# Batch 0's k and v: 128 partitions, one queue, and a compact kv

## The chip, the cores and the metric

The kernel runs on one core of a Trainium2 chip. The metric is the time of one execution on the device in microseconds (us); lower is better. Three executions of the kernel before took 262.84, 264.09 and 265.5 us, so the median is 264.09 us.

The engines of the core are named as the profile names them: PE multiplies matrices (PEld is its weight load), DVE works on vectors, ACT applies functions elementwise, POOL is a general engine, SP only issues transfers. DMA moves data between the device memory and the on-chip memory. A DMA that SP or ACT issues goes to a hardware queue (q1 for SP in the profile), one that POOL issues goes to the software queue q0; a cast from float32 to bfloat16 on the way is done only in POOL's DMAs here.

## The reference

For each of 8 batches and 8 heads with 576 tokens and head size 64, a linear attention is computed, and its output of 512 columns goes through a normalised two-layer block:

```python
q_s = softmax(q, over the 64 columns of a token)
k_s = softmax(k, over the 576 tokens)
kv  = einsum('bhsd,bhse->bhde', k_s, v)        # 64 x 64 for each head
x   = einsum('bhsd,bhde->bhse', q_s, kv)       # heads side by side: 576 x 512
xn  = (x - mean) / sqrt(var + 1e-6) * g_ln
out = x + relu(xn @ w_ch1) @ w_ch2             # 512 -> 2048 -> 512
```

Inputs and output are float32. The kernel multiplies in bfloat16 and accumulates in float32.

## The kernel before

The tokens of a batch are cut into four tiles of 128 (t = 0 to 3) and a remainder of 64; the remainders of all eight batches form a ninth block. Batches 1 to 7 and that ninth block are pipelined: while PE runs the two layers of one batch, the other engines prepare the attention of the next. The order of the instructions on every engine is written out by hand: a list of main steps (`mlp_steps`) with weights, and side steps with a place among them (`run`). Each engine works its own list strictly in order.

Batch 0 has nothing to hide behind, so `first_batch` (L957) handles it by itself:

- SP issues q's tiles 0 and 1 (L978) and then k in four transfers of two heads (L980). k and v stand on P0 = 96 partitions, with T0 = 6 tokens on each.
- POOL waits in its list at `gate` (L1004) for q's first transfer. Then it issues v with a cast (three DMAs, L1006), q's tiles 2 and 3 (two DMAs, L970 through L1010), and then the weights: the first 512 columns of w_ch1 in two halves of its rows (L1013), the other three blocks of 512 columns (L99), w_ch2, and batch 1's inputs. All of these share the software queue.
- PE keeps itself busy with products of a tile of zeros (`warm`, L867: 34, later 11 more).
- q's tiles 0 and 1 are exponentiated (L220), normalised on DVE (L229, L274, L923) and transposed through PE (L928) into `eqT`.
- k is exponentiated on ACT for two heads at a time (L293). Products with a column of ones give the sums of k (`z0_mm`, L306); products with v for two heads at a time give a 128 x 128 block with two useful 64 x 64 blocks on its diagonal (`kv0_mm`, L321). DVE divides by the sums and masks with `diag` in one instruction, which also sums the rows (L322); `mbc` spreads the sum divided by -512 over 128 columns (L327, L331).
- `xT_mm` (L342) gives x for tiles 0 and 1 already transposed and with the mean taken off: a direct part (one product of 128 rows for each pair of heads j) and a mean part (products with `mbc`). `xT_out` (L351, L353) scales it by g and writes `xnT`, the input of the first layer.
- The first layer (`mm1_part`, L520) starts with 8 products of the upper rows of w_ch1 (ko 0, 1) and goes on with 8 of the lower rows (ko 2, 3), each set over m = 0 to 3 for tiles 0 and 1. Side steps stand between: at 2 and 4 `q0_rest` for tiles 2 and 3 (sums of q by PE, L940, then x through PE with all of kv of batch 0, L414), at 6 the transpose of tile 2's normalised x (`xn_pT`, L928 and L932).

What matters for the order is that ACT's list holds exp of q's tiles 2 and 3 (L1039, L1040), then the scalings of `xT_out` 2 and 3.

Of the kernel before, what the change touches and what calls it, by code (L numbers as in the profile page):

```python
# [15 lines left out]
ALU = mybir.AluOpType  # L16
# [4 lines left out]
def kernel(  # L21
# [49 lines left out]

    ident = const.tile([P, P], BF16)
    eps_ln = const.tile([P, 1], FP32)
    gate = const.tile([P, 4], FP32)
    ones = const.tile([P, 1], BF16)
    junk = const.tile([P, 256], BF16)
    scrap = const.tile([P, 512], BF16)
    bones = const.tile([P, 2], BF16)
    ones_w = const.tile([P, P], BF16)
    diag = const.tile([P, P], FP32)  # L80
    mbc = const.tile([P, NP, P], BF16)
# [9 lines left out]
    vr = const.tile([P, 2, H, VW], BF16)  # L91
    vm = const.tile([P, 2, T, H, VW], BF16)

    w1_src = moe_w_ch1.rearrange("(ko ki) n -> ki ko n", ki=P)
    w2_src = moe_w_ch2.rearrange("(ko ki) n -> ki ko n", ki=P)

# [190 lines left out]
    kvbox = {}  # L287

    def exp_k0(j):
        hs = slice(2 * j, 2 * j + 2)  # L290
        if j == 0:
            eks[0] = raw.tile([P, T0, H, D], BF16, tag="kt", name="ek0", bufs=1)
        nc.scalar.activation(  # L293
            eks[0][0:P0, :, hs, :].rearrange("p t h d -> p h t d"), raws[0][0][0:P0, hs], AF.Exp
        )

    def k0_mm(j, t):
        hs = slice(2 * j, 2 * j + 2)
        return eks[0][0:P0, t, hs, :], raws["v0"][0:P0, hs, t, :], P

    def z0_mm(j):

        if j == 0:
            kvbox["z0"] = mm_ps.tile([P, NP], FP32, tag="m", name="z0")
        for t in range(T0):
            nc.tensor.matmul(  # L306
                kvbox["z0"][:, j : j + 1], k0_mm(j, t)[0], ones[0:P0],
                start=(j == 0 and t == 0), stop=(t == T0 - 1), skip_group_check=True,
            )

    def recip_z():
        kvbox["rz"] = sml.tile([P, NP], FP32, tag="rzk", name="rzk")
        kvbox["sum"] = sml.tile([P, NP], FP32, tag="lnv", name="kvs")
        nc.vector.reciprocal(kvbox["rz"], kvbox["z0"])

    def kv0_mm(j):
        pool, tag = (att_ps, "a") if j < 2 else (mm_ps, "m")
        pkv = pool.tile([P, P], FP32, tag=tag, name="pkv")
        for t in range(T0):
            lhsT, rhs, w = k0_mm(j, t)  # L320
            nc.tensor.matmul(pkv[:, 0:w], lhsT, rhs, start=(t == 0), stop=(t == T0 - 1))  # L321
        nc.vector.scalar_tensor_tensor(  # L322
            kv_sb[:, 0, j, :], in0=pkv, scalar=kvbox["rz"][:, j : j + 1], in1=diag,
            op0=ALU.mult, op1=ALU.mult, accum_out=kvbox["sum"][:, j : j + 1],
        )
        if j < NP - 1:
            nc.scalar.activation(  # L327
                mbc[:, j], ones_w, AF.Copy, scale=kvbox["sum"][:, j : j + 1]
            )
        else:  # L330
            nc.vector.tensor_scalar_mul(  # L331
                out=mbc[:, j], in0=ones_w, scalar1=kvbox["sum"][:, j : j + 1]
            )

    def xT_mm(j, kh):

        if j == 0:
            pobox["T", kh] = mm_ps.tile([P, 2, 2, P], FP32, tag="m", name="pxT")
        ops = [(kv_sb[:, 0, j, :], j % 2)] if j // 2 == kh else []
        ops += [(mbc[:, j], i) for i in range(2)]  # L340
        for n, (lhsT, i) in enumerate(ops):
            nc.tensor.matmul(  # L342
                pobox["T", kh][:, i], lhsT, eqTs[0][:, 0:2, j, :],
                start=(j == 0 and n == 0), stop=(j == NP - 1 and n >= len(ops) - 2),
                skip_group_check=True,
            )
# [8 lines left out]
    halves = (slice(0, 64), slice(64, P))  # L355

    def kv_pairs(b, ts=range(T + 1)):

# [598 lines left out]
    def first_batch():  # L957

        nc.scalar.preload_act_table_set("natural_log_exp_and_others")
        raws[0] = (  # L960
            mlp.tile([P, H, T0, D], FP32, tag="hT", name="kt0", bufs=1), None,
            raw.tile([P, H, T, D], FP32, tag="qt", name="qt"),
        )
        k0, _, q0 = raws[0]
        v0 = mlp.tile([P, H, T0, D], BF16, tag="hs", name="v0", bufs=1)
        raws["v0"] = v0

        def load_q0(t, tn, eng):
            ts = slice(t, t + tn)
            eng.dma_start(  # L970
                q0[:, :, ts],
                q[0, :, 0:SM, :].rearrange("h (p t) d -> p h t d", t=T)[:, :, ts],
            )

        def src0(x, h0, hn):
            return x[0, h0 : h0 + hn].rearrange("h (p t) d -> p h (t d)", t=T0)

        load_q0(0, 2, nc.sync)  # L978
        for h0 in range(0, H, 2):
            nc.sync.dma_start(  # L980
                k0[0:P0, h0 : h0 + 2].rearrange("p h t d -> p h (t d)"), src0(k, h0, 2)
            )
# [6 lines left out]
        nc.vector.memset(ones, 1.0)  # L989
# [3 lines left out]
        nc.vector.memset(ones_w, -1.0 / DM)  # L993
        nc.vector.memset(diag, 0.0)
        for ps in halves:
            nc.vector.memset(diag[ps, ps], 1.0)
        nc.vector.memset(kv_sb[:, 1:B], 0.0)
# [4 lines left out]
        make_identity(nc, ident)  # L1002
        nc.gpsimd.tensor_copy(out=ident_f, in_=ident[0:KO1, 0:KO1])
        nc.gpsimd.tensor_copy(out=gate, in_=q0[:, 1, 0, 0:4])  # L1004
        for h0, hn in ((0, 4), (4, 2), (6, 2)):
            nc.gpsimd.dma_start(  # L1006
                v0[0:P0, h0 : h0 + hn].rearrange("p h t d -> p h (t d)"), src0(v, h0, hn)
            )
        for t in range(2, T):
            load_q0(t, 1, nc.gpsimd)  # L1010
        for kh in range(2):
            ks = slice(2 * kh, 2 * kh + 2)
            nc.gpsimd.dma_start(w1_sb[:, ks, 0:512], w1_src[:, ks, 0:512])  # L1013
# [12 lines left out]
        warm(11)  # L1026
        eq_pT(0, 1, nc.vector)
        for j in range(NP):
            exp_k0(j)
            z0_mm(j)  # L1030
            if j == NP - 2:
                g_columns()
        recip_z()
        kv0_mm(0)
        kv0_mm(1)
        kv0_mm(2)
        xT_mm(0, 0)
        kv0_mm(3)
        exp_qt(0, 2)  # L1039
        exp_qt(0, 3)  # L1040
        xT_mm(1, 0)
        xT_mm(2, 0)
        xT_mm(0, 1)
        xT_mm(3, 0)
        xT_out(0)
        xT_out(1)
        eq_pT(0, 2, nc.scalar)
        xT_mm(1, 1)
        xT_mm(2, 1)
        eq_pT(0, 3, nc.vector)  # L1050
        xT_mm(3, 1)
        xT_out(2)
        xT_out(3)

    def q0_rest(t):
        z_q(0, t)
# [20 lines left out]
    def load_batch(b, parts=(2, 0), after=None):  # L1077
# [14 lines left out]
    with tc.manual_schedule(  # L1092
# [11 lines left out]
        def po_x(c, t):  # L1104
            for i in range(NP):
# [85 lines left out]
```

## Time and profile before

| What | Value |
|---|---|
| Median of three executions | 264.09 us (262.84 to 265.5) |
| Profiled execution, its own time | 265.09 us |
| Its span, first to last instruction | 263.3 us |
| PE busy | 254.8 us (97%) |
| DVE, ACT, POOL busy | 223.6, 177.7, 101.3 us |
| TensorE clock granted from 4.8 us to 264.2 us | full speed |
| DMA | 45.04 MB, mean 171 GB/s |

The span is less than the execution's own time by 1.8 us, which lie around the instructions. Times in a view count from the start of the span. A view by line names the line of the kernel and the tile that is written and read; a number behind x is how many instructions were merged; square brackets give how long the engine was idle before and what ended the wait. Busy shares say little here, because the first 20 us have other limits than the rest. The profile counts a casting DMA by the bytes that it writes, half of what it reads.

### The profile page before, as it was taken

The page shows a single profiled execution, that of the slowest core. Times are in us where ns is not written, and L with a number is a line of the kernel's source. Part 1 is how long each engine was busy: PE and PEld are TensorE (multiplying, and loading weights), DVE is VectorE, ACT ScalarE, POOL GpSimd, SP SyncE. Part 2 cuts the span into 40 slices and gives each one's busy share as a digit, 9 for nine tenths or more (in the row PEclk, how much of TensorE's full clock was granted, in tenths as well). Part 3 has the DMA queues.
Part 4 walks back from the last instruction along what each step waited for, and adds up shares of the span by engine and source line. Part 5 has one row for each costly group of instructions (what it writes and reads, how often), then busy time and mean ns, then how long its engine had stood idle before and what let it go on. Part 6 is the DMA issues. An engine that isn't in the chain of part 4 may idle for free.

```text
span 263.3 us, 7326 instructions
## 1 busy us (share of the span) xinstructions
PE 254.8 (97%) x2904; PEld 218.2 (83%) x2907; DVE 223.6 (85%) x544; ACT 177.7 (67%) x348; POOL 101.3 (38%) x158
## 2 busy tenths in 40 slices
PE   8879999999999999999999999999999999999993
PEld 6669854788888788888888888888988888888883
DVE  6658996998998999799979997999799979967873
ACT  4646972797887677688768866886688386638500
POOL 3952238240099306920790089008200910090000
PEclk9999999999999999999999999999999999999999
DMA  6999999987699997699879968998902540323014
GB/s 201 249 201 208 353 218 242 267 235 243 146 131 192 332 162 142 194 309 118 136 207 305 115 125 254 268 113 147 289 9 42 122 159 4 60 64 120 2 40 120
DMA packets 82618, 45.04 MB, mean 171 GB/s; under 512 B 58196, under 2 KB 79192, under 8 KB 82584
## 3 DMA queue, kind: packets, MB, share of 16 engines
q0 software_dynamic: 32464, 21.76, 44.8%
q1 hardware_dynamic: 49488, 22.29, 37.3%
q10 hardware_dynamic: 632, 0.53, 0.7%
q8 instruction: 22, 0.36, 0.6%
q14 instruction: 12, 0.10, 0.1%
HBM read 36.70 MB, written 9.44 MB: 175 GB/s over the span
## 4 chain that ended last, share of the span: by engine, by line
PE 91%; DMA 5%; POOL 2%; DVE 0%; issue 0%; DVEq 0%
PE ba L604 21%; PE bx L762 20%; PE bb L762 10%; PE ph L520 8%; PE bb L604 6%; PE be L604 5%; PE bc L604 5%; PE pc L556 5%; PE bc L762 5%; DMA w_raw<-in_moe_w_ch_dram 3%; PE pkv L371 2%; DMA qt<-in_q_dram 2%; PE po L403 2%; PE ptr L928 1%; PE po L414 1%; POOL v L1006 1%
## 5 line engine op out<-in xcount | busy, mean ns | idle before, releaser
L604 PEld LDWEIGHTS <-hs 128*128 128x128 bf16 x512 | 49.6, 98 | 6.3 <-issue 0.3
L269 POOL TENSOR_TENSOR tq<-xnT 128x256 bf16<-128x256 bf16 x30 | 20.1, 671 | 83.4 <-DMA xnT<-xn 42.5
L762 PEld LDWEIGHTS <-w_raw 128*128 128x128 bf16 x480 | 46.5, 98 | 6.4 <-issue 0.8
L604 PEld LDWEIGHTS <-hT 128*128 128x128 bf16 x392 | 37.6, 98 | 4.2
L762 PEld LDWEIGHTS <-w1g 128*128 128x128 bf16 x360 | 34.8, 98 | 4.2
L762 PE MATMUL bx<-tq,w_raw 128*128 128x256 bf16 x240 | 31.6, 273 | 0.3 <-DVE bb L793 0.3
L604 PE MATMUL ba<-w_q,hs 128*128 128x256 bf16 x256 | 30.6, 273 | 0.0
L786 ACT COPY bc<-bx 128x512 f32<-128x512 f32 x30 | 16.7, 596 | 19.1 <-PE bx L762 19.1
L427 ACT ACTIVATE scrap<-x,mv 128x512 bf16<-128x512 bf16 x32 | 23.1, 723 | 4.7 <-DVE mv L457 4.5
L793 DVE TENSOR_TENSOR bb<-bx,s 128x512 f32<-128x512 f32 x30 | 19.4, 694 | 7.7 <-ACT s L790 5.1
L804 ACT ACTIVATE hT<-bb 128x512 bf16<-128x512 f32 x30 | 16.4, 595 | 10.8 <-PE bb L762 10.8
L587 DVE TENSOR_TENSOR hs<-hT 128x1024 bf16<-128x1024 bf16 x32 | 21.3, 672 | 0.5 <-ACT hT L804 0.5
L796 DVE TENSOR_TENSOR hT<-bx,s 128x512 bf16<-128x512 f32 x30 | 19.3, 684 | 2.9 <-PE bx L762 2.7
L804 ACT ACTIVATE hT<-bc 128x512 bf16<-128x512 f32 x30 | 16.3, 595 | 7.8 <-PE bc L762 7.8
L229 DVE TENSOR_REDUCE zq<-eq 128x16 f32<-128x1024 bf16 (+1 forms) x20 | 20.7, 1050 | 0.6 <-ACT eq L220 0.5
L269 POOL TENSOR_TENSOR tq<-xnT,tq 128x256 bf16<-128x256 bf16 x30 | 20.0, 668 | 1.1
L449 DVE SCALAR_TENSOR_TENSOR x<-po,rq 128x256 bf16<-128x256 f32 x48 | 17.5, 420 | 1.4 <-PE po L403 1.4
L790 ACT COPY s<-bb 128x512 f32<-128x512 f32 x30 | 16.6, 623 | 0.0
L520 PE MATMUL ph<-xnT,w_raw 128*128 128x256 bf16 (+1 forms) x144 | 15.0, 261 | 1.5 <-DMA w_raw<-in_moe_w_ch_dram 1.5
L804 ACT ACTIVATE hT<-bx 128x512 bf16<-128x512 f32 x30 | 16.4, 610 | 0.0
L762 PE MATMUL bx<-xnT,w1g 128*128 128x256 bf16 x120 | 16.2, 273 | 0.0
L762 PE MATMUL bb<-xnT,w_raw 128*128 128x256 bf16 x120 | 15.8, 273 | 0.0
(156 smaller groups left out, 537.0 us busy)
## 6 DMA issues: line engine op xcount, KB each, us to landing
out_dram<-ot POOLq DMA_DIRECT2D x30, 256.0 KB, 4.6
kt<-in_k_dram SPq DMA_DIRECT2D x5, 1024.0 KB, 12.5
qt<-in_q_dram SPq DMA_DIRECT2D x4, 1024.0 KB, 8.6
qt<-in_q_dram POOLq DMA_DIRECT2D x2, 1024.0 KB, 13.2
kt<-in_k_dram POOLq DMA_DIRECT2D x2, 1024.0 KB, 14.2
vm<-in_v_dram POOLq DMA_DIRECT2D x16, 128.0 KB, 13.1
qt<-in_q_dram SPq DMA_DIRECT2D x3, 512.0 KB, 5.9
w_raw<-in_moe_w_ch_dram POOLq DMA_DIRECT2D x3, 512.0 KB, 11.8
```

The costliest lines, as they stand in the source:

```text
L229: nc.vector.reduce_sum(eqs[c][1][:, ts], eqs[c][0][:, ts], axis=AX.X)
L269: nc.gpsimd.tensor_tensor(out=dst[:, t], in0=x[:, t], in1=y[:, t], op=ALU.subtract)
L427: nc.scalar.activation(scrap, x[:, t], AF.Square, bias=mv[:, t, 0:1], scale=-float(DM), accum_out=mv[:, t, 1:2],)
L449: nc.vector.scalar_tensor_tensor(x[:, t].rearrange("p (i two d) -> p i two d", two=2, d=D)[:, :, half], in0=pobox[c, t][half], scalar=1.0, ...
L520: nc.tensor.matmul(ph[:, m % 2, at : at + tn], (w1g if c else w1_sb)[:, ko, m * P : (m + 1) * P], xnTs[c][:, t0 : t0 + tn, ko, :], start=( ...
L587: nc.vector.tensor_tensor(out=dst, in0=x, in1=y, op=op)
L604: nc.tensor.matmul(hbox[bank][:, t, cs], lhsT, rhs[:, cs], start=first and (own or t == 0) and k == 0, stop=k == KH - 1, skip_group_check= ...
L762: nc.tensor.matmul(dst[:, q], lhsT, rhs, start=first and q == 0 and ko == 0, stop=ko == 1, skip_group_check=True)
L786: nc.scalar.copy(at[g, "c"], at[g, "x"])
L793: nc.vector.tensor_tensor(out=at[g, "b"], in0=at[g, "x"], in1=at[g, "s"], op=ALU.add)
L796: nc.vector.tensor_tensor(out=h_out(g, 1, 1), in0=at[g, "x"], in1=at[g, "s"], op=ALU.add)
L804: nc.scalar.activation(h_out(g, odd, half), at[g, name], AF.Relu)
```

## The change

- k and v of batch 0 are laid out as 2 heads x 64 partitions with T0 = 9 tokens each, so on all 128 partitions, one pair of heads in a transfer. v arrives as float32 (`v0f`) and is cast on the chip: three pairs on ACT, one on DVE (`cast_v0`).
- SP issues everything of batch 0 on its one queue: q's tiles 0 and 1, k (4), v (4), then q's tiles 2 and 3 together. POOL's `gate` now waits for the last transfer of k, and its next DMA is the first of the weights.
- v has a 65th column of ones, so the products give the sums of k as well; `z0_mm` is gone. A product now takes one head's 64 partitions and 64 columns: 72 instead of 24.
- The three pairs of the first group are evicted together, the fourth by itself (`kv0_out`), to a compact `kvc` and the scaled sums `kvm`. ACT copies `kvc` to the diagonal of `kv_sb` later (`kv0_copy`). `diag`, `ones_w` and `mbc` are gone.
- x's direct part is two products of 64 rows for each pair (`xT_kv`); the mean part reads one column of `kvm` 128 times (`xT_mean`).
- `g_columns` stands right behind the 34 warm products. The clearing of `kv_sb` for batches 1 to 7 goes from DVE to POOL. The transpose of q's tile 2 is evicted by DVE, and tile 3's transposes stand in the first layer at 1. ACT's list becomes: exp of q (2), exp of k (4), casts (3), first copy of kv, exp of q's tile 2, `xT_out` 1, exp of q's tile 3, `xT_out` 3, second copy of kv.
- For batches 6 and 7 q and k are loaded in two halves; before, this was so for batch 7's q alone.

```diff
-    T0 = 6
-    P0 = S // T0
+    T0 = 9
...
+    def cast_v0(j, eng):
+        dst, src = raws["v0"][:, j, :, 0:D], raws["v0f"][:, j]
...
+    groups = (slice(0, NP - 1), slice(NP - 1, NP))
+
+    def kv0_mm(j):
...
         for t in range(T0):
+            for ps in halves:
+                nc.tensor.matmul(
+                    kvbox[n][ps, j - js.start], eks[0][ps, j, t], raws["v0"][ps, j, t],
...
+    def kv0_out(n):
...
+        nc.vector.reciprocal(rz, pkv[:, :, D])
+        if num > 1:
+            nc.vector.tensor_mul(kvc[:, js], pkv[:, :, 0:D], rz.to_broadcast([P, num, D]))
+            nc.vector.reduce_sum(total, kvc[:, js], axis=AX.X)
+        else:
+            nc.vector.scalar_tensor_tensor(
+                kvc[:, js.start], in0=pkv[:, 0, 0:D], scalar=rz, in1=ones_f,
+                op0=ALU.mult, op1=ALU.mult, accum_out=total,
+            )
+        nc.vector.tensor_scalar_mul(out=kvm[:, js], in0=total, scalar1=-1.0 / DM)
+
+    def kv0_copy(n):
+        for ps in halves:
+            nc.scalar.copy(kv_sb[ps, 0, groups[n], ps], kvc[ps, groups[n]])
+
+    def xT_kv(j):
...
+        for ps in halves:
             nc.tensor.matmul(
+                pobox["T", kh][ps, i], kvc[ps, j], eqTs[0][ps, 0:2, j, :],
...
+    def xT_mean(j, kh):
+        for i in range(2):
             nc.tensor.matmul(
+                pobox["T", kh][:, i], kvm[:, j : j + 1].to_broadcast([P, P]),
+                eqTs[0][:, 0:2, j, :], start=False, stop=(j == NP - 1), skip_group_check=True,
             )
...
-        if i < 2:
+        if i % 2 == 0:
             nc.vector.tensor_scalar_mul(out=dst, in0=src, scalar1=g_one[:, i : i + 1])
...
         load_q0(0, 2, nc.sync)
+        for x, dst in ((k, k0), (v, v0f)):
+            for j in range(NP):
+                nc.sync.dma_start(
+                    dst[:, j : j + 1].rearrange("p j t d -> p j (t d)"), src0(x, j, 1)
+                )
+        load_q0(2, 2, nc.sync)
...
+        nc.gpsimd.memset(kv_sb[:, 1:B], 0.0)
+        nc.gpsimd.tensor_copy(out=gate, in_=k0[:, NP - 1, 0, 0:4])
...
-        nc.gpsimd.tensor_copy(out=gate, in_=q0[:, 1, 0, 0:4])
-        for h0, hn in ((0, 4), (4, 2), (6, 2)):
-            nc.gpsimd.dma_start(
-                v0[0:P0, h0 : h0 + hn].rearrange("p h t d -> p h (t d)"), src0(v, h0, hn)
-            )
-        for t in range(2, T):
-            load_q0(t, 1, nc.gpsimd)
...
         warm(34)
+        g_columns()
...
+        for j, eng in enumerate((nc.scalar, nc.scalar, nc.vector, nc.scalar)):
+            cast_v0(j, eng)
+        for j in range(NP):
+            kv0_mm(j)
+            if j < NP - 1:
+                warm(2)
             if j == NP - 2:
+                kv0_out(0)
+        kv0_out(1)
+        for j in range(NP - 1):
+            xT_kv(j)
+        for j in range(NP):
+            xT_mean(j, 0)
+        kv0_copy(0)
         exp_qt(0, 2)
         xT_out(0)
         xT_out(1)
+        xT_mean(0, 1)
+        xT_mean(1, 1)
+        xT_mean(2, 1)
+        xT_kv(3)
+        xT_mean(3, 1)
+        exp_qt(0, 3)
         xT_out(2)
         xT_out(3)
+        eq_pT(0, 2, nc.vector)
+        kv0_copy(1)
...
-            hn = H // 2 if (b, which) == (B - 1, 2) else H
+            hn = H // 2 if b >= B - 2 else H
...
+                (1, lambda: eq_pT(0, 3, nc.vector)),
                 (2, lambda: (q0_rest(2), x_fast(0, 2), x_normed(2))),
```

More of the change, by code (lines that the diff above doesn't have):

```diff
@@ L78 @@
     bones = const.tile([P, 2], BF16)
-    ones_w = const.tile([P, P], BF16)
-    diag = const.tile([P, P], FP32)
-    mbc = const.tile([P, NP, P], BF16)
+    ones_f = const.tile([P, D], FP32)
+    gate = const.tile([P, 4], FP32)
+    kvm = const.tile([P, NP], BF16)
+    kvc = const.tile([P, NP, D], BF16)
     g_one = const.tile([P, KO1], FP32)
@@ L92 @@
     vm = const.tile([P, 2, T, H, VW], BF16)
+    halves = (slice(0, 64), slice(64, P))
     w1_src = moe_w_ch1.rearrange("(ko ki) n -> ki ko n", ki=P)
@@ L289, in exp_k0 @@
     def exp_k0(j):
[L290 removed]
         if j == 0:
[L292 to L305 removed]
+            eks[0] = raw.tile([P, NP, T0, D], BF16, tag="kt", name="ek0", bufs=1)
@@ new lines, in exp_k0 @@
+        nc.scalar.activation(eks[0][:, j], raws[0][0][:, j], AF.Exp)
+    def cast_v0(j, eng):
+        dst, src = raws["v0"][:, j, :, 0:D], raws["v0f"][:, j]
+        if eng is nc.scalar:
+            nc.scalar.copy(dst, src)
+        else:
+            nc.vector.tensor_copy(out=dst, in_=src)
+    groups = (slice(0, NP - 1), slice(NP - 1, NP))
+    def kv0_mm(j):
+        n, js = next((n, js) for n, js in enumerate(groups) if js.start <= j < js.stop)
+        if j == js.start:
+            kvbox[n] = att_ps.tile([P, js.stop - js.start, VW], FP32, tag="a", name="pkv")
+        for t in range(T0):
+            for ps in halves:
+                nc.tensor.matmul(
+                    kvbox[n][ps, j - js.start], eks[0][ps, j, t], raws["v0"][ps, j, t],
+                    start=(t == 0 and j == js.start), stop=(t == T0 - 1), skip_group_check=True,
+                )
@@ L306, in z0_mm @@
+    def kv0_copy(n):
+        for ps in halves:
+            nc.scalar.copy(kv_sb[ps, 0, groups[n], ps], kvc[ps, groups[n]])
+    def xT_kv(j):
+        kh, i = divmod(j, 2)
+        if i == 0:
+            pobox["T", kh] = mm_ps.tile([P, 2, 2, P], FP32, tag="m", name="pxT")
+        for ps in halves:
             nc.tensor.matmul(
-                kvbox["z0"][:, j : j + 1], k0_mm(j, t)[0], ones[0:P0],
-                start=(j == 0 and t == 0), stop=(t == T0 - 1), skip_group_check=True,
-            )
@@ L311, in recip_z @@
[L311 to L341, printed above, removed]
+                pobox["T", kh][ps, i], kvc[ps, j], eqTs[0][ps, 0:2, j, :],
+                start=(i == 0), stop=False, skip_group_check=True,
+            )
+    def xT_mean(j, kh):
+        for i in range(2):
@@ L992, in first_batch @@
         nc.vector.memset(bones[64:P, 1:2], 1.0)
[L993 to L997, printed above, removed]
+        nc.vector.memset(ones_f, 1.0)
+        nc.vector.memset(v0[:, :, :, D:], 1.0)
+        nc.vector.memset(kv_sb[:, 0], 0.0)
+        make_identity(nc, ident)
+        nc.gpsimd.tensor_copy(out=ident_f, in_=ident[0:KO1, 0:KO1])
+        nc.gpsimd.memset(kv_sb[:, 1:B], 0.0)
+        nc.gpsimd.tensor_copy(out=gate, in_=k0[:, NP - 1, 0, 0:4])
         nc.vector.memset(vr, 0.0)
```

52 lines of the change are left out of this document (15 added, 37 removed).

## The prediction

> **What bounds the kernel now.** I first read the chain of work that ended last, in its first 36 us (start, us, what):
>
> ```profile
> 0.74 4.38 DMA qt<-in_q_dram
> ...
> 5.17 0.19 POOL gate L1004
> 5.36 2.07 POOL v L1006 x3
> 7.43 1.84 POOL qt L970 x2
> 9.27 0.64 POOL w_raw L1013
> 9.91 8.81 DMA w_raw<-in_moe_w_ch_dram
> 18.72 0.05 issue
> 18.77 0.61 PE ph L520 x4
> 19.38 0.22 PE ptr L928 x4
> ...
> 21.79 11.37 PE ph L520 x112
> ```
>
> The start is a chain of transfers: q lands at 5.12, the gate opens, POOL issues v and q's late tiles, then the weights, and PE waits for their second half until 18.72. After that the chain is PE without a break (91% of the span is PE). So the change can act only ahead of that point, and every microsecond by which PE's list moves there moves the end. My marker is PE's transposes of tile 2's normalised x, at 19.22 in the time line of PE. The same time line shows what preceded:
>
> ```profile
> 15.16 0.38 PE L342 MATMUL pxT<-eqT,mbc 128*128 128x256 bf16 x2
> 15.76 0.61 PE L520 MATMUL ph<-xnT,w_raw 128*128 128x256 bf16 x4 [0.22 <-DMA w_raw<-in_moe_w_ch_dram]
> ...
> 17.07 0.38 PE L414 MATMUL po<-kv_sb,eqT 128*128 128x128 bf16 x4
> 18.77 0.61 PE L520 MATMUL ph<-xnT,w_raw 128*128 128x256 bf16 x4 [1.32 <-DMA w_raw<-in_moe_w_ch_dram]
> ```
>
> The attention of batch 0 had been done by 17.5; it waited 1.3 us for weights. Third, the DMA view by queue (packets, MB, share), in 3 to 4 us (q's early tiles, 512-byte packets), 14 to 16.5 us (weights) and, from the middle of the kernel, 90 to 92.5 us, where both queues have work:
>
> ```profile
> q1 hardware_dynamic: 621, 0.32, 107.8%
> ```
>
> ```profile
> q0 software_dynamic: 512, 0.50, 122.0%
> ```
>
> ```profile
> q1 hardware_dynamic: 586, 0.60, 86.2%
> q0 software_dynamic: 586, 0.09, 46.9%
> ```
>
> From these: a 512-byte packet of q takes one of the 16 engines 16 x 1 / 621 = 26 ns, a weight packet (1 KB written) 16 x 2.5 / 512 = 78 ns. And when both queues have work they take turns packet by packet, 586 to 586, whatever the sizes: SP's packets hold 1 KB there, POOL's 0.15 KB.
>
> **The transfers.** Before, v and q's late tiles stood ahead of the weights in one queue. Now they are SP's, and the weights are POOL's: order becomes sharing.
> - k: 288 KB on 96 partitions land every 1.01 us (the exponentials wait for them at 7.20 and 8.22; 293 GB/s in 5 to 7 us). 128-partition transfers with 1 KB rows show 385 GB/s on the same queue in 64.5 to 66.5 us. That gives 0.77 us a transfer; the bounds are 0.77 and 1.01. I take 0.77, the row with 128 partitions. k's last part then lands at 5.12 + 4 x 0.77 = 8.2, v's at 9.0, 9.7, 10.5, 11.3. Before, v landed by 12.5.
> - Gate and issue: 0.2 us after 8.2, so the weights are issued from 8.4 (before: 9.22). Between v's first issue on POOL at 5.29 and the queue's first packets at about 7.7 there were 2.4 us, so weight packets start at 10.8.
> - q's late tiles: k's last packets went 1.2 us before k's landing (7.9 against 9.15), so SP's queue turns to q at about 10.1. 1024 packets of 512 bytes are 64 for each engine. In the 0.7 us until 10.8 some 27 go; the other 37 take turns with weights: 37 x (26 + 78 ns) = 3.85 us, to 14.65. The landing follows 1.2 us later at best; the two weight halves landed 3.0 us apart though their packets need 1.25, so the last engine can lag 1.75 more. That bounds q's landing **L by 15.85 and 17.6**; I take 16.8, about the middle. Before, q's last tile was there when ACT asked at 13.14.
> - The weights' first half then lands about 14.5 and the second by 17.5 at the latest; neither is last.
>
> [...] This trace shows turns of one recorded packet each. [...]
>
> **The data path up to x.**
> - `g_columns` moved: DVE's two copies now wait for a product behind the 34 warm ones, which end at 6.6, instead of standing at 10.24. Behind them wait the sums of q, the normalising, the transposes' evictions and the DVE cast: the chain that began at 5.80 begins at 7.24, 1.44 later, and its last eviction ends at 11.36.
> - Casts: ACT 0.62 each by its 128x512 rows; v's pairs 0, 1 and 3 are cast by 9.7, 10.4 and 12.0. DVE's cast of pair 2 follows 11.36: between 0.35 (128x512 without PSUM) and 0.75; 0.6 gives 12.0.
> - Products: `z0_mm` goes (24 x 25 ns, 0.6 us, beside the wait for v). The 64x65 products of later batches take 10 in 0.16 us (L371), so a pair's 18 take 0.3 and its drain 0.2. Pair 2 is ready at 12.5.
> - Evictions: reciprocal 0.2, product of 192 columns 0.38 (L379: 0.42 for 256), sum of 192 columns 0.35 (L229: 0.69 for 512), scaling 0.2; for pair 3 0.2 + 0.35 + 0.2. That is 1.9 us, to 14.4. Gone are four L322 (0.43) and the four `mbc` (0.25 to 0.4), which had been spread beside the products.
> - x: mean part of pair 3 by 14.65, `xT_out` 0 on DVE at 15.2; ten more products of 0.11 keep PE until 15.8. Before: 15.3. So on this path alone the first layer could start at 15.85 instead of 15.76, with its second half no longer waiting for weights.
> - POOL's clearing of 3584 columns: 0.20 for 128 columns against 0.10 for one (the memsets at its start) is 0.8 ns a column, 2.9 us, from 1.6 to 4.5, hidden by the wait for k. By POOL's tensor rows (671 ns for 256) it would be 9.4 us and end at 11. I take the memset row. DVE's 1.55 us were hidden too.
> - Splitting loads of batches 6 and 7 adds three issues of 0.5 us on SP, which has slack of tens of us: nothing.
>
> **Where it meets.** ACT works in order: exp of q's tile 2 waits for L, and behind it stand `xT_out` 1, exp of tile 3, `xT_out` 3 and the second copy of kv. Counted from L: exp 0.6, `xT_out` 1 0.5, exp 0.6, `xT_out` 3 0.4, two copies 0.4: kv of batch 0 is complete at L + 2.5. PE's list waits with it: tile 2's x (L414) at L + 2.55 to 2.9 with its drain, then DVE's 0.74 and 0.35 (x, normalised x): the marker's transposes at **L + 4.1**. In between PE fits 4 products, tile 3's sums and x, and 4 more (1.4 us), so it idles. L = 15.1 would leave 19.22 unchanged. With L = 16.8 the marker is at 20.9, 1.7 us later.
>
> The sum on the profiled execution: 263.3 + 1.7 = 265.0 of span, with 1.8 around it 266.8. That execution lay 1.0 above the median, so against the median: 264.1 + 1.7 = **265.8 us**.
>
> **Rivals.**
> 1. q's late tiles get through first: weight packets come later than 2.4 us after issue, or q's turns are larger. Speaks for it: 0.9 us more of head start would clear all 64 packets (1.7 us alone), and the 2.4 us from issue to first packet are known from one case. Against: 586 to 586. Then L is below 14.3, the exps are off the path and the marker is bound by the data path: PE goes 15.85, second copy of kv 16.7, x of tile 2 by 17.1, normalised 18.4. That is 0.8 earlier: **263.3 us**, not slower. Decides from L = 15.1. Little more can come: the next weight block was needed at 21.8 and landed at 20.6.
> 2. The transfers do not gain from 128 partitions (1.01 us each). k lands at 9.15 as before, weight packets start at 11.75, v's end at 12.0, so all 64 packets of q take turns: 12.0 + 6.7 + 1.2 = 19.9. The marker is at 24.0, **268.9 us**. For it: v's packets are as large as k's. Against: 385 GB/s.
> 3. POOL's clearing is slow (9.4 us): the gate passes at 11, weights start at 13.4, q is through; the second half of the weights lands 2 us later than before, while the data path is early: **265.5 us**.
>
> **How the numbers follow.** Forecast 0.5, rival one 0.3, rival two 0.13, rival three 0.07. A difference of 1% (2.6 us) is about what a measurement of this kernel can tell from no change, since three executions spread over 2.7. The forecast's own range is 264.8 to 267.6, from L = 15.85 to 17.6 and 1 us of the executions' spread. The range reaches from 262.8 (rival one with its half of the spread) to 268.5, leaving out half of rival two and the tails. Slower by over 1% needs L above 17.7: 0.17 of the forecast's 0.5, rival two's 0.13 and 0.06 of the rest: 0.36. Faster by over 1% would need a second gain on top of rival one: 0.12. Within 1%: 0.52.
>
> **What would show it.** In the profile after: the weights' issue near 8.4; k's exponentials 0.77 apart; ACT's exp of q's tile 2 with an idle time ended by DMA qt, near 16.8; PE's x of tile 2 (L417 there) waiting for ACT's copy; the marker near 20.9. In the DMA view from 11 to 14.5, q1 and q0 with like packet counts. Wrong if ACT's exp does not wait for q, if the weights still end PE's wait, or if PE is not continuous after 24 us.

## The result

| What | Before | After |
|---|---|---|
| Median of 20 executions each, same chip | 263.80 us (262.48 to 265.50) | 265.20 us (264.55 to 267.09) |
| Ratio, 95% interval | | 1.0068 (1.0049 to 1.0087) |
| Profiled execution, its own time | 265.09 us | 265.16 us |
| Its span | 263.3 us | 263.4 us |

The changed kernel is slower by 0.7%. The ratio is that of the comparison and not the quotient of the two medians (1.0053); it leaves out executions of more than 1.5% above the fastest of the same kernel. The two profiled executions take the same time, so they alone cannot show where 1.4 us went: the profiled execution of before lay 1.3 us above its median. The changed kernel's 20 executions fall into two groups: 13 of them between 264.55 and 265.86 us, and 7 between 266.6 and 267.1 us, all seven with a mean granted clock of 0.994.

### The profile page after: what moved, and what is told of

The parts are those of the page before. It is cut to its first block, busy times and chain, and to the rows that moved or that the text cites. A ratio compares the mean times of both kernels' runs of the same rounds, so it can differ in the third digit from the quotient of the medians.

```text
span 263.4 us, 7405 instructions
## 1 busy us (share of the span) xinstructions
PE 254.7 (97%) x2938; PEld 217.4 (83%) x2941; DVE 222.4 (84%) x541; ACT 178.4 (68%) x351; POOL 100.5 (38%) x154
## 4 chain that ended last, share of the span: by engine, by line
PE 68%; DMA 21%; issue 4%; DVE 2%; POOL 2%; SPq 1%; POOLq 0%
PE bx L765 19%; PE ba L607 18%; PE bb L765 9%; DMA vt<-in_v_dram 7%; DMA qt<-in_q_dram 5%; PE bb L607 5%; PE bc L607 5%; PE be L607 5%; PE bc L765 4%; DMA w_raw<-in_moe_w_ch_dram 3%; DMA xnT<-xn 3%; DMA kt<-in_k_dram 2%; PE po L406 2%; PE pkv L374 1%; POOL tq L268 1%
## 5 line engine op out<-in xcount | busy, mean ns | idle before, releaser
L765 PE MATMUL bx<-tq,w1g 128*128 128x256 bf16 x120 | 15.7, 273 | 0.0
```

Of the source, the lines that this page charges most:

```text
L765: nc.tensor.matmul(dst[:, q], lhsT, rhs, start=first and q == 0 and ko == 0, stop=ko == 1, skip_group_check=True)
```

## The profile after

The chain of work that ended last is no longer PE's alone. First its shares by engine on the page, then three of its pieces in order of time (start, us, what):

```profile
PE 68%; DMA 21%; issue 4%; DVE 2%; POOL 2%; SPq 1%; POOLq 0%
```

```profile
2.81 5.95 DMA kt<-in_k_dram
10.53 8.47 DMA w_raw<-in_moe_w_ch_dram
...
70.46 7.80 DMA xnT<-xn
```

The last piece is new: followed back from the end, the chain leaves PE near 78 us and goes to a transposing DMA of batch 2's normalised x. The time line of PE shows the start and that place (start, us, engine, line, operation; in brackets the idle time before):

```profile
8.49 0.40 PE L931 MATMUL ptr<-ident,eq 128*128 128x128 bf16 x4 [1.88 <-DVE eq L926]
...
15.90 0.38 PE L523 MATMUL ph<-xnT,w_raw 128*128 128x256 bf16 x2
...
18.71 0.40 PE L931 MATMUL ptr<-ident,xn 128*128 128x128 bf16 x4
...
78.40 1.03 PE L765 MATMUL bx<-xnT,w1g 128*128 128x256 bf16 x8 [0.90 <-DMA xnT<-xn]
```

The marker, the transposes of tile 2's normalised x, is at 18.71 instead of 19.22: 0.5 us earlier, not 1.7 later. The first layer starts at 15.90 and no longer waits for weights. Then 0.9 us are lost at 77.5, far behind the stage that the change is about. New at the start is 1.88 us of idle PE ahead of the transposes of q.

The step that the forecast rested on did not happen. ACT's time line, and the DMA view by queue from 9.8 to 11.3 us (packets, MB, share):

```profile
12.97 0.71 ACT L333 COPY kv_sb<-kvc 64x192 bf16<-64x192 bf16 x2 [0.62 <-DVE kvc L322]
13.70 0.63 ACT L219 ACTIVATE eq<-qt 128x512 bf16<-128x512 f32 x1
```

```profile
q1 hardware_dynamic: 846, 0.53, 109.8%
q0 software_dynamic: 2, 0.00, 0.8%
```

The exponential of q's tile 2 starts right behind the copy of kv and waits for nothing. In the trace's packet records the first packet of q's late tiles goes at 9.72 and the first of the weights at 11.24. By then 737 of q's 1024 packets had gone; the rest went until 12.78, and q landed at 13.13.

## The experiments

Times are medians of 12 executions where nothing else is said. "Before" is the kernel before on the same chip in the same comparison. The clock's moments are from the trace's records of the granted clock.

### The kernels again

Neither kernel has an edit here.

> The kernel before, unchanged, for a second profiled execution and the granted clock of each of its executions. If the profiled execution of before was an odd one (it lay 1.3 us above its median of 263.8), the second profile shows the second half of the first weights earlier than 18.72 us, tile 2's transposes near 18.2 and a time near 263.8. If it was typical, 18.72 and 19.22 come again. Clock theory: all executions of before at a mean granted clock of 0.999 to 1.0. Against it: some at 0.994, as in the changed kernel.

> The changed kernel, unchanged, beside it. Expected again: ratio to before 1.005 to 1.009, about a third of the executions near 266.8 us with a mean clock of 0.994 and the others near 264.7. In the profile, PE's wait for the transposed x of batch 2 (0.9 us near 77.5 us) if that is a property of the kernel; none if it was chance in one execution.

Measured: before 264.00 us (262.85 to 265.44), ratio to the other executions of the same kernel 1.0008 (0.9979 to 1.0037). The changed kernel 266.97 us over 11 executions, ratio 1.0075 (1.0035 to 1.0116); four at 264.4 to 264.6 us and seven at 266.8 to 268.8 us with a mean clock of 0.992 to 0.994 (the long group). With the first comparison that makes 14 of 31 executions. Of 114 executions of the kernel before in the four comparisons here, 6 have a mean clock under 0.995, so the claim that it never does so was too strong.

The second profile of before (PE's time line) took 263.35 us, which is nearer to the medians of before (263.5 to 264.0) than the 265.09 of the first:

```profile
15.14 0.60 PE L520 MATMUL ph<-xnT,w_raw 128*128 128x256 bf16 x4
...
16.86 0.61 PE L520 MATMUL ph<-xnT,w_raw 128*128 128x256 bf16 x4
17.32 0.40 PE L928 MATMUL ptr<-ident,xn 128*128 128x128 bf16 x4
```

The weights' halves land at 14.60 and 16.81 here (15.71 and 18.72 in the first profile), PE does not wait for them, and the marker is at **17.32**. Against this execution the changed kernel's 18.71 is 1.39 later. So 19.22, from which the prediction counted, lies 1.9 above it. This execution is itself 0.45 to 0.65 us shorter than the medians of 263.80 and 264.00; if all of that lay ahead of the marker, an execution at the median would have it at 17.8 to 18.0 (an estimate).

The second profile of the changed kernel was one of the long executions. In the view by windows, behind a window and its length stand the busy time of PE, PEld, DVE, ACT and POOL, then the granted clock, the DMA engines' share and GB/s:

```profile
3.30:6.70 3.40, 3.40 (x18) 2.42 (x17) 0.11 (x1) 2.04 (x4) 1.27 (x1) 1.00 1.08 397
6.80:10.10 3.30, 1.42 (x14) 1.06 (x13) 1.98 (x6) 2.74 (x5) 2.46 (x5) 1.00 1.04 401
10.20:13.50 3.30, 3.30 (x35) 2.43 (x32) 1.86 (x6) 0.68 (x1) 3.30 (x5) 0.50 1.17 239
```

In the second row PE is busy for 1.42 of 3.30 us, because the 1.88 us of idle time fall into it whole; in the third the clock is at half. The records of the clock change at 6.74, 10.16 and 13.57 us, 3.41 apart. The transposes of q begin at 9.89 instead of 8.49, the marker is at 21.54 instead of 18.71, and the wait for the transposed x (1.62 us) is there again. (At 268.75 us it is the longest of the eleven; the median of the seven long ones is 267.16.) The moment from which full speed is granted differs by execution: 3.88 and 6.74 in the two profiles of the changed kernel, 4.78 and 4.17 in those of before. The 1.88 us of idle time ahead of the half clock are 0.55 of the 3.41 us from one record to the next.

### The load of batch 3's v, moved far

```diff
-        s += [(66, lambda: load_v(3, True))]
+        s += [(97, lambda: load_v(3, True))]
```

> The changed kernel with the load of batch 3's v (POOL, issued at 71.1 us) moved behind POOL's differences for batch 2, to about 79 us, so that it no longer runs beside the transposes of batch 2's normalised x. Transpose theory: the landing of the second transpose goes from 78.3 to about 74, PE's 0.9 us wait at 77.5 goes, and the time falls by 0.5 to 0.9 us, to 263.8 to 264.2 in executions at full clock. Rival (the transposes are late because their packets share engines with something else): the wait stays, time within 0.2 us of the changed kernel's. The share of executions at 0.994 should not change in either.

Measured: 268.26 us over 6 executions, ratio 1.0166 (1.0119 to 1.0213); three at full clock take 266.6 to 267.5 us, three with a mean clock of 0.991 or 0.992 take 269.1 to 269.4. The landing moved as expected (75.02, 3.1 us after the issue instead of 7.8) and the wait for it went; but POOL's differences `tq`, no longer behind the issue of v, started at 71.10 instead of 73.83 and ran beside DVE's sums of the hidden layer. Time lines of DVE and PE:

```profile
72.18 2.23 DVE L590 TENSOR_TENSOR hs<-hT 128x1024 bf16<-128x1024 bf16 x2
74.33 2.23 DVE L590 TENSOR_TENSOR hs<-hT,hs 128x1024 bf16<-128x1024 bf16 x2
```

```profile
74.47 1.48 PE L607 MATMUL ba<-w_q,hs 128*128 128x256 bf16 x12 [0.47 <-DVE hs L590]
77.22 1.91 PE L607 MATMUL be<-w_sb,hs 128*128 128x256 bf16 x16 [1.27 <-DVE be L636]
```

Two of these sums take 2.23 us instead of 1.28, POOL's differences beside them 0.92 to 1.11 instead of 0.67, and PE waits 1.74 us for DVE. The issue of v had kept POOL off DVE in that stretch.

### PE's idle time filled

```diff
         warm(34)
         g_columns()
+        warm(14)
```

> The changed kernel with 14 more warm products behind the products of g, which fill PE's idle time of 1.9 us from 6.6 to 8.5 us. Clock theory (that idle time lets the granted clock fall for a few us in a third of the executions): no execution at 0.994, median 264.7, highest below 265.9, some 0.5 us lower in the median. Rival (the clock falls for another reason, or the sparse products from 8.5 to 15 us do it): a third of the executions stay near 266.8. In a profile at full clock both expect no change, as the products end at about 8.2, ahead of the transposes of q at 8.5.

Measured: 265.26 us (264.65 to 265.57), ratio 1.0060 (1.0037 to 1.0082). None of the 12 executions has a clock under 0.997 and none is above 265.6. The window from 5.30 to 8.60, in which PE idled before, is full:

```profile
5.30:8.60 3.30, 3.30 (x30) 2.80 (x29) 1.22 (x5) 2.88 (x5) 0.41 (x2) 1.00 1.03 392
```

The long group is gone, so the idle time is its cause. But the rest stays 1.7 us above before: in this profile full speed came at 5.23 us, the transposes began at 9.15 and the marker is at 19.71. Filling the gap does not bring back the time at which DVE starts.

### The products of g back at their old place

```diff
         warm(34)
-        g_columns()
...
         eq_pT(0, 1, nc.vector)
+        g_columns()
```

> The changed kernel with the products of g and DVE's two copies back behind the eviction of q's second transpose, as in the kernel before. Theory: behind the 34 warm products g's products wait for the moment at which full clock is granted (3.9 us in one profile, 6.7 in another: the transposes of q began at 8.49 and 9.89), while the kernel before begins them at 7.36 and 7.51 whatever the clock does. Then here the transposes begin near 7.4 in any execution, PE's idle time ahead of them is 0.8 to 1.0 us, no execution has a mean clock of 0.994 with 267 us, and the executions lie between 264.2 and 265.2. Rival: the order of DVE makes no difference to the clock: a third to a half stay near 267. Since v's last transfer lands at 11.65 anyway, I expect no start of the first layer below 15.5.

Measured: **263.90 us** (263.26 to 264.30), ratio to before 0.9986 (0.9965 to 1.0007); before 263.94. No execution in a long group, and the rest about 1 us shorter than the changed kernel's at full clock (median 263.9 against 264.8). PE's time line:

```profile
7.06 0.39 PE L931 MATMUL ptr<-ident,eq 128*128 128x128 bf16 x4
...
18.31 0.40 PE L931 MATMUL ptr<-ident,xn 128*128 128x128 bf16 x4
```

Full speed came at 5.76 us here, later than in the first profile of the changed kernel, and yet the transposes begin 1.43 us earlier. This one edit takes back the whole loss: behind the 34 warm products, the products of g wait for the clock. In the first profile of the changed kernel the warm products start 213 ns apart up to 3.8 us and 109 ns apart from 3.96 us on, in that of before 213 up to 4.66 and 109 from 4.84 on; the moment differs by execution, and DVE's whole list waits behind the two copies of g. The marker, 18.31, is still 1.0 later than in the second profile of before; 0.4 us of that come back behind the marker (239.77 us from there to the end of PE, against 240.16), and why is open.

### The same part alone, in the kernel before

```diff
         warm(34)
+        g_columns()
...
             z0_mm(j)
-            if j == NP - 2:
-                g_columns()
```

> The kernel before with one part of the change alone: the products of g and DVE's copies moved right behind the 34 warm products. Theory: the transposes of q now begin 1 to 2.5 us later (8.5 to 9.9, by the clock's phase) instead of at 7.4; executions split as those of the changed kernel do: a third to a half with a window at half clock and some 2 to 3 us longer (266 us), the others up to 1 us longer than before. Rival (the loads and evictions of the change make the split): time within 0.3 us of before and no second group.

Measured: 264.19 us, ratio 1.0029 (0.9999 to 1.0060). Four of 12 executions are long (266.5, 266.6, 266.7 and 268.1 us, clock 0.990 to 0.994), eight lie between 263.7 and 264.7. PE's time line has the same gap:

```profile
8.95 0.40 PE L928 MATMUL ptr<-ident,eq 128*128 128x128 bf16 x4 [1.88 <-DVE eq L923]
```

The move makes the second group without any other part of the change. The eight others hardly move (median 264.06 against 263.94; the profiled one, with its marker at 18.45, is the longest of them): in that profile the transposes of q are 1.6 us later than in the second profile of before, the first layer (15.96) 0.8 and the marker 1.1. So part of the delay is covered on the way; why the median of the eight shows almost none of it is open.

### The weights released early

```diff
-        nc.gpsimd.tensor_copy(out=gate, in_=k0[:, NP - 1, 0, 0:4])
+        nc.gpsimd.tensor_copy(out=gate, in_=k0[:, 0, 0, 0:4])
```

> The changed kernel with the gate on the first of k's transfers (lands 5.43) instead of the last (8.76), so that the weights' packets meet v's and q's. If packets of two queues take turns one for one, as the prediction had it: weight packets from about 8.0, v's last 28 packets per engine take turns with them, v's last landing 11.65 goes to 14, q's late tiles land at 19 to 20.7 instead of 13.13, ACT's exponential of tile 2 waits for q, the marker goes from 18.7 to 23 to 25, the time to 269 to 271. If q's and v's packets pass weights in larger turns: v within 0.7 us of 11.65, q by 15, marker below 20, time at most 266.5.

Measured: 270.45 us over 4 executions, ratio 1.0232 (1.0187 to 1.0278). From 12 to 16 us both queues have work, in the DMA view:

```profile
q0 software_dynamic: 580, 0.57, 83.6%
q1 hardware_dynamic: 576, 0.30, 35.6%
```

and ACT's time line:

```profile
20.95 0.63 ACT L219 ACTIVATE eq<-qt 128x512 bf16<-128x512 f32 x1 [4.43 <-DMA qt<-in_q_dram]
```

As many packets of one queue go as of the other, q lands at 20.93, ACT waits 4.43 us, and the marker is at 24.75, 3.8 behind the landing. That is the mechanism of the forecast, once both queues have packets to send; the changed kernel did not come to it. (The profiled execution also has a window at half clock, and the weights' packets came 4.1 us after their issue, not 2.4, so v lost about 1 us and not 2.4.) Larger turns of q and v than of the weights, the other case of the expectation, would show as unequal counts; the row, 580 to 576 recorded packets, is not that. Equal counts say that the turns are of equal length, not how long they are.

### The load of batch 3's v, moved by two sums

```diff
-        s += [(66, lambda: load_v(3, True))]
+        s += [(78, lambda: load_v(3, True))]
```

> The changed kernel with DVE's clearing that releases the load of batch 3's v placed two sums later (about 1.2 us), so that POOL issues it 1.8 us behind the issue of the second transpose of batch 2's x instead of 0.6, with nothing else of POOL's order moved. Transpose theory: that transpose lands 3.0 to 3.9 us after its issue instead of 5.1 to 7.8, PE's wait of 0.9 us (1.6 in the second profile) near 77.5 goes, and executions at full clock fall from 264.4 to 265.2 to about 263.7 to 264.3; the share of executions at 0.994 stays. Rival (the transpose is late because PE's 16 KB instruction fetch falls into its issue): the landing stays at 5 us or more and the wait stays above 0.5 us.

Measured: 265.49 us, ratio 1.0074 (1.0050 to 1.0098), two of 12 executions long. The mechanism came out, the gain did not. The transposes by tile (the row of SP's queue, then their time to landing) and PE's time line:

```profile
L276 SPq DMA_TRANSPOSE xnT<-xn x2: 1253/1418/1584, 67.0 to 70.8; - x2
...
DMA to landing us min/median/max: 3.0/3.1/3.1
```

```profile
77.67 1.04 PE L765 MATMUL bx<-xnT,w1g 128*128 128x256 bf16 x8
78.78 1.03 PE L765 MATMUL bb<-tq,w_raw 128*128 128x256 bf16 x8
```

An instruction fetch (queue q8, one packet of 16 KB) falls into the issue here too, at 70.75, and the landing is still 3.0 us after it; so the load of v is what holds the transpose's last pieces. PE no longer waits for the transpose, but its second group starts 1.11 us behind the first, where 0.87 is the rule (`bx` to `bb` in the changed kernel): 0.24 us go to POOL's differences, which stand behind the later issue. From the marker on, this profile needs 240.10 us against 240.63 of the changed kernel, 0.5 less, but its marker is at 19.03, 0.3 later. The executions at full clock (265.0 to 266.4) show no gain. Why is open.

### ACT's list, the evictions, and the split of the loads

The remaining four start from the run with g back. The first moves the exponential of tile 3 and the second copy of kv ahead of `xT_out` 1:

```diff
         exp_qt(0, 2)
+        exp_qt(0, 3)
+        kv0_copy(1)
         xT_out(0)
         xT_out(1)
...
-        exp_qt(0, 3)
         xT_out(2)
...
-        kv0_copy(1)
```

The second has a like list on ACT, forms two groups of two pairs, and puts the first eviction and eight mean products ahead of the second eviction's result:

```diff
-    groups = (slice(0, NP - 1), slice(NP - 1, NP))
+    groups = (slice(0, 2), slice(2, NP))
...
-            if j == NP - 2:
+            if j == 1:
                 kv0_out(0)
```

The third undoes the split of the loads:

```diff
-            hn = H // 2 if b >= B - 2 else H
+            hn = H // 2 if (b, which) == (B - 1, 2) else H
```

> The run with g's products back at their old place (263.9 us), and on ACT the exponential of q's tile 3 and the second copy of kv moved ahead of xT_out 1, into the 1.2 us in which ACT waits there (13.63 to 14.80). Theory (the marker is held by ACT's serial list behind the late eviction of kv: second copy of kv ends at 16.86, x of tile 2 waits for it): x of tile 2 starts about 0.4 us earlier, the marker goes from 18.31 to 17.9, the time falls by 0.2 to 0.4 us. Rival (PE's order of mean products holds it, PE being busy from 13.2 to 17): nothing changes by more than 0.1 us.

> The same, with the evictions of kv by pairs 0, 1 and then 2, 3 instead of 0 to 2 and then 3, so that eight of the sixteen mean products and the first eviction come before v's last pair is there, and ACT's list as in the run beside it. Theory (the change's two evictions stand in one stretch behind the last v, with 14 mean products of 0.11 us behind them): the first layer starts at 14.9 instead of 15.5, the marker goes from 18.3 to 17.4 to 17.6, the time falls to 263.0 to 263.3, some 0.5 us below the kernel before. Rival (DVE's longer chain takes it back: the cast of pair 2 and the first eviction meet): marker above 18.0, time within 0.2 us of 263.9.

> The run with g's products back, and the loads of batches 6 and 7 whole again as in the kernel before (three issues of SP fewer). Expected by all: within 0.2 us of 263.9, no wait of PE in the last three batches either way.

Measured: 263.43 us, 0.9991 (0.9969 to 1.0013); 263.59 us, 0.9991 (0.9974 to 1.0009); 264.03 us, 1.0010 (0.9990 to 1.0029), with before at 263.78. None differs from before by more than the interval. The markers are at 18.14, 17.68 and 18.37; the first of them moved by 0.17 us of the 0.4 expected. PE's time line of the two groups:

```profile
14.84 0.27 PE L523 MATMUL ph<-xnT,w_raw 128*128 128x256 bf16 x1
15.35 0.27 PE L523 MATMUL ph<-xnT,w_raw 128*128 128x256 bf16 x1 [0.24 <-ACT xnT L358]
...
17.68 0.40 PE L931 MATMUL ptr<-ident,xn 128*128 128x128 bf16 x4
```

The profile gains 0.63 us at the marker over the run with g back, most of what was expected, but the median only 0.3, and the ratio nothing that can be told from chance. A wait of 0.79 us for the transpose, at 76.9, is in the profile of the first of them and in neither of the other two. The split of batches 6 and 7 is worth nothing measurable.

The last puts four more products into a place of two warm ones:

```diff
-            if j < NP - 1:
+            if j < 2:
                 warm(2)
...
+            if j == 2:
+                xT_kv(0)
+                xT_kv(1)
```

> The run with two evictions of two pairs (263.59 us, marker 17.68), with the four products of compact kv for pairs 0 and 1 put in the place of the two warm products ahead of pair 3's products. Theory (PE's list of mean products, without a gap from 11.8 to 14.8 there, is what now starts the first layer): that list ends 0.3 us earlier, the first layer starts at 14.5, the marker is at 17.3, the time 263.2 to 263.4, 0.4 us below the kernel before. Rival (the wait for xT_out 1 on ACT and for DVE's x takes its place): marker 17.6 or later, time unchanged.

Measured: 263.63 us, ratio 0.9994 (0.9973 to 1.0016). The first layer starts at 14.81 and the marker is at 17.65: the rival was right in its sign. The second product of the first layer waits 0.24 us for ACT's `xT_out` 1, at 15.32; that this wait alone holds the marker is not shown. The profiled execution, 264.7 us, has the wait for the transpose again, 1.29 us. No version here beats the kernel before beyond its interval.

## Why the prediction was right in its number and wrong in its cause

The time (265.8 predicted, 265.2 measured) and the sign came out, by other terms than those of the sum. The agreement is luck: the one term that made the forecast slower, the late landing of q, did not occur, and the loss that was measured comes from a term that the prediction held to be covered.

| In the profiles, us | Before | Before, again | After | After, again | g back | Two groups |
|---|---|---|---|---|---|---|
| Full clock from | 4.78 | 4.17 | 3.88 | 6.74 | 5.76 | 6.14 |
| Transposes of q | 7.51 | 7.36 | 8.49 | 9.89 | 7.06 | 7.24 |
| First layer | 15.76 | 15.14 | 15.90 | 18.74 | 15.51 | 14.84 |
| Marker | 19.22 | 17.32 | 18.71 | 21.54 | 18.31 | 17.68 |
| End of PE less marker | 240.11 | 240.16 | 240.63 | 241.38 | 239.77 | 239.74 |

1. **"q's late tiles land at 16.8", the +1.7 us: failed, by the 2.4 us from issue to first packet.** The prediction took this time for a delay that runs from POOL's issue, so that 0.7 us lay between the first packet of q's late tiles and the first of the weights. The packet records show something else:

| us | After | After, again | g back | Two groups | Weights released early |
|---|---|---|---|---|---|
| POOL issues the weights | 8.94 | 7.76 | 8.54 | 7.87 | 5.49 |
| First packet of q's late tiles | 9.72 | 9.68 | 9.76 | 9.77 | 9.77 |
| First packet of the weights | 11.24 | 11.20 | 11.27 | 11.28 | 9.59 |
| q's late tiles landed | 13.13 | 11.96 | 12.51 | 12.07 | 20.93 |

In all ten profiles whose gate is on k's last transfer, the weights' first packet stands 1.51 us behind q's first, whether POOL issued them at 7.76 or at 8.94. One engine's 64 packets in 1.51 us are 24 ns a packet, and from 10.6 to 11.2 us the first profile has 385 of them on 16 engines, 25 ns each; so by this estimate the weights began when the first DMA engine was through with its packets of q. The others fit: in the first profile 223 packets of the weights went before q's last one, and at 78 ns each the engines that had completed q had time for about 227 (an estimate from the times of their completions). The 2.4 us read from the kernel before were such a wait too: its software queue's first packet (7.77, and 7.96 in the second profile) comes within 0.02 us of the first completion (a packet of 4 bytes) of k's last transfer (7.76 and 7.96). So the weights came 3.4 us after their issue in the second profile, where they were issued 0.6 us earlier than predicted, as the first rival had it ("weight packets come later than 2.4 us after issue"); in the first profile, where k's third and fourth transfers were late, it was 2.3. The sharing on which the sum rested did not take place. At the start, only the run with the weights issued at 5.49 has like counts of both queues from 12 to 16 us (580 to 576 packets, against 700 to 35 in the first profile of the changed kernel; marker at L + 3.8, where L + 4.1 was predicted). Why the software queue waits in the one case and not in the other is open. The landing "1.2 us later at best" was too long as well: q landed 0.35 us behind its last packet (12.78), 0.42 in the early release, and in the kernel before k landed 0.8 us behind its last packet, which went at 8.37 and not at 7.9. The prediction gave the far side of its mechanism 0.3.
2. **The baseline failed.** "That execution lay 1.0 above the median" was taken as an offset on everything. It was in this very stage: the weights' second half at 18.72 instead of 16.81. In the second profile an instruction fetch (queue q8) goes at 14.27 and not, as in the first, at 16.69 beside the last packets of that half; that this delays it is argued, not shown. With the marker of the second execution, 17.32, the first rival's 18.4 would have been a loss of 1.1 us, not a gain of 0.8.
3. **"`g_columns` moved: 1.44 later", and then covered: failed.** The size was near (the transposes of q are 1.0 later in the first profile and 2.4 in the second), but it is no constant: it follows the moment at which full clock is granted. It was not covered either: with the copies back the executions at full clock are 1 us shorter. And the idle time that it leaves on PE costs a window at half clock: the long group, 14 of 31 executions, lies 2.1 and 2.7 us above the others (264.8 to 266.9 and 264.5 to 267.2, the medians in the two comparisons). A window of 3.41 us at half clock lowers the mean clock over 265 us by 0.006, to the 0.994 of these executions; the window itself was seen in one of them, and without the idle time none of 12 was long. This one edit is the measured loss: 1.0068 with it, 0.9986 (0.9965 to 1.0007) without; in the kernel before, the move alone costs less (1.0029).
4. **The data path's sums held**: the transfers 0.68 to 0.77 us apart (0.77 predicted) but for k's third and fourth in the first profile (1.65 and 0.93; 0.76 and 0.77 in the second), casts 0.67 and 0.75 (0.62, 0.6), POOL's clearing 3.07 (2.9), the evictions 12.36 to 14.11, 1.75 (1.9), the first layer at 15.90 (15.85). That the first layer came out to 0.05 us is partly chance, as k landed 0.6 us later than in the sum. The second rival (1.01 a transfer) and the third (slow clearing) fell.
5. **Where the earlier data went.** v's last transfer lands at 11.65 (12.54 and 11.94 before), but from there to the first layer it takes 4.25 us against 3.2 in the second profile of before, and from there to the marker 2.81 against 2.18: the evictions stand in one stretch behind the last v, then the mean products, then ACT's list. Two groups of two pairs regained most of that in the profile.
6. **"Wrong if PE is not continuous after 24 us": it was not.** In five profiles with v's issue 0.6 us behind that of the second transpose and no wait, it landed 4.9 to 5.6 us after its issue; in four others, 7.7 to 8.5 us, and PE waited 0.8 to 1.6 us. In both profiles of before and in the one with g moved, POOL issued v 1.3 us behind it and it landed after 3.0. That the load of v does this is shown by the two runs that moved it; why POOL takes 0.4 us from DVE's clearing to the issue where before it took 1.1 is open (there the profile names DVE's sum `hs` as what ended POOL's wait). The wait is in two of the profiles with g back as well, whose medians equal that of before, so it explains little of the 1.4 us. Both of these profiled executions lie 1.1 us above their medians, so the wait may cost that much where it occurs; how many executions have it no run shows.
7. **The split of the loads: nothing**, as predicted.

## What to carry to other kernels

Do not put small work that a long list waits for behind filler products that run before full clock: their end moves with the clock from execution to execution, and the list with it (full clock from 3.88 and 6.74 us, the transposes of q at 8.49 and 9.89, in the two profiles of the changed kernel). Before a profiled execution serves as a baseline, compare its own time with the median, and ask in which stage the difference lies; a second profile would have moved the marker by 1.9 us. A transfer that is issued earlier or later meets other transfers and other engines far behind its stage, so the whole of PE's time line is read for new waits. A delay read from one trace may be a wait for something else: look for what ended at the moment at which it ended.

## What the hardware showed that was not expected

- A gap of 1.88 us, far shorter than the 3.41 us between two changes of the clock, was followed by 3.41 us at half clock: 1.42 us busy of 3.30 in the second profile of the changed kernel; 1.80 of 3.40 (from 5.70 to 9.10 in the run with v moved far) was not. From record to record, the two windows ahead of half clock (in the second profile of the changed kernel and in the early release) hold 1.53 and 1.54 us busy of 3.41; later windows with 1.65 and 1.68 us kept full clock.

```profile
5.70:9.10 3.40, 1.80 (x16) 1.37 (x13) 1.49 (x5) 3.34 (x7) 1.47 (x3) 1.00 1.04 409
9.20:12.50 3.30, 3.12 (x58) 2.39 (x59) 3.03 (x7) 1.16 (x2) 3.30 (x6) 1.00 1.12 298
```

- DVE's bfloat16 sums of two operands and POOL's differences slow each other: in the run with v moved far DVE's four sums start 1.08 us apart instead of 0.6, and POOL's differences take 0.92 to 1.11 us instead of 0.67. One behind the other, a sum of 0.69 us and a difference of 0.67 would take 1.36 us; here such a pair took 1.08. By what they slow each other is not shown.
- A transposing DMA behind which POOL issues a load 0.6 us later lands up to 5.5 us late (8.5 us after its issue in the second profile of the changed kernel, 3.1 with the load issued later): its data packets had gone by 74.0 in the changed kernel, but the 16 completions came between 75.4 and 78.3, among v's packets.
- The software queue's first packet started when the first DMA engine was through with the hardware queue's packets, in thirteen of the fourteen profiles (at the kernel's start, and for those with SP's one queue by the estimate above; the early release is the fourteenth). In the first profile of before it goes at 7.77 and the first completion at 7.76; in that of the changed kernel it goes at 11.24, 1.51 us behind the first of q's 64 packets for each engine.
